# An explicit table of all operations in place of a list scheduler, in an attention and MLP kernel

## The chip, the core and the metric

The kernel runs on one core of one Trainium2 chip. The core has a matrix engine (TensorE, PE in the profile; its weight loads are PEld), a vector engine (VectorE, DVE), a scalar engine (ScalarE, ACT), a general one (GpSimd, POOL) and an engine that here only issues DMAs (SyncE, SP). Each works through its own queue in order. The metric is the time of one execution in microseconds of device time; lower is better.

## What is computed

Attention with a bias that a small network makes from the relative position, and then a two-layer MLP with a leaky activation over the concatenated heads. All is float32, and the constants in front of the random inputs are left out here:

```python
scores = scale * np.matmul(q, k.transpose(0, 1, 3, 2))          # B 4, H 8, S 576, D 64
rel = (pos[:, None] - pos[None, :]).astype(np.float32)
x = (np.log1p(np.abs(rel)) / np.log1p(np.maximum(pos[:, None], 1.0)))[..., None]
bias = np.maximum(x @ w1 + b1, 0.0) @ w2                         # hidden 32, one column per head
attn = softmax(scores + bias.transpose(2, 0, 1)[None])
out = np.matmul(attn, v)
...
h = x @ w_in                                                     # 2304 x 512 @ 512 x 2048
g = np.maximum(h, 0.0) + alpha * np.minimum(h, 0.0)
return g @ w_out                                                 # 2304 x 2048 @ 2048 x 512
```

## The kernel before

The program first makes a list of 2816 operations and then puts them in order. Each operation is one closure that issues one or a few instructions, with the engines on which it may run and an assumed duration for each, the buffers that it reads and writes, and a key.

The parts are these. Thirty-six bias tiles (`bias_tile`, "bias t"): for 4 x 4 positions each, four relu rows of 576 columns (L491 on DVE, L494 on ACT or L497 on POOL, tag "H"), a block of 16 matmuls with them (L506), an evacuation with scaling (L516 on ACT or L519 on DVE, tag "ev") and a store to a scratch array in DRAM. Eight weight pairs (`weights`, "w fp"): loads of 512 KB, unpacking of the input's 64-bit words with one shift (L678) and two combining steps on DVE (L681), maxima (L685, L686), casts to a high half in float16 (L700, L706, tag "wh") and the low half (L404). Turned q and k (`qk_turn`), the rows of v (`v_rows`). Thirty-two attention units (`unit`): scores (L613, L614), the row minimum on DVE (L808), the exponential on ACT (L811), the sum plus a small constant (L814, tag "ep"), its reciprocal (L816), and then for batch 0 a scaling (L831, tag "no"), turning on PE (L840) and evacuation (L850, tag "at"), for batches 1 to 3 a float16 high half (L821 on POOL, L822 on ACT, tag "nh"), the low half (L824) and a transposing DMA on SP into the tile `at`; then the product with v (L861, L869). Nine chunks of 256 tokens of the MLP (`chunk`, `layer_pair`): per pair of 128 columns the first layer (L939, 24 matmuls), two scalings (L946 on ACT, L947 on DVE), a cast (L950, tag "g0"), a subtraction (L951, tag "g1") and the second layer (L958); at the end of a chunk the output scaling (L920, L921, tag "mo") and the store.

Data are split into a high and a low float16 half, and three products of the halves stand for one product, so that most matmuls come in threes.

`Planner.plan` is a list scheduler: it goes through simulated time, and whenever an engine is free it takes the ready operation with the least key that finds free buffers, with assumed durations and an assumed slowing of DVE and POOL by one another (`SLOW`). The keys are the program's own plus an offset per part, all in the dictionary `ORDER`. The result fixes engine, buffer and place of every operation. `tc.manual_schedule` then issues them in that order, and waits on semaphores are made from the dependences. While the first MLP call isn't reached, PE gets fillers in planned gaps of over 600 ns: matmuls of 512 columns on a constant, into the tile H (L1012; 175 of them).

What sets the work around the change is thus the place of an operation in its engine's queue, the wait of its first instruction, and the buffer it was given: the small classes are two tiles S (and O as a third) and one tile A and H in PSUM, two float16 tiles `a` and two tiles `at`.

## Time and profile before

| | us |
|---|---|
| median of 3 runs | 737.98 (737.81 to 738.19) |
| profiled execution | 735.5 |
| its span | 733.7 |
| PE busy, of the span | 688.6 (94%) |
| DVE busy | 546.5 (74%) |
| ACT busy | 416.2 (57%) |
| POOL busy | 158.0 (22%) |

The span runs from the first instruction to the end of the last work; what lies around it makes up the rest of the profiled execution's time. Matmul records overlap, so a busy PE is not a PE at its peak. The share of an engine over the whole span is a mean over stages with different limits, so the views below are taken by stretch: busy time in windows, groups of instructions by line of code with the mean of one, who waited for whom, and the order in time. A wait that was for several engines stands under the one that came last.

### The profile page before, as it was taken

What the parts mean: (1) busy time and instruction counts of PE and PEld (TensorE: products, weight loads), DVE (VectorE), ACT (ScalarE), POOL (GpSimd) and SP (SyncE); (2) the same over time, 40 slices, a digit from 0 to 9 for tenths busy, and PEclk for the clock granted to TensorE, in tenths of its full rate; (3) what the DMA queues carried; (4) which work ended last, traced back from release to release, by engine and by line L of the source; (5) the groups of instructions that cost most, each with busy time, mean ns of one, the idle gap of its engine ahead of it and who ended that gap; (6) DMA issues with size and microseconds to landing.
All of it is one profiled execution on the core that took longest, in us unless ns stands there. A gap on an engine that the chain in (4) does not pass through costs nothing.

```text
span 733.7 us, 14984 instructions
## 1 busy us (share of the span) xinstructions
PE 688.6 (94%) x5508; PEld 421.8 (57%) x5508; DVE 546.5 (74%) x1267; ACT 416.2 (57%) x821; POOL 158.0 (22%) x191
## 2 busy tenths in 40 slices
PE   8888888988999999998999999999989999999997
PEld 3443334545656675655666666666656656666764
DVE  6999999899778987888987688777666775233332
ACT  3787777767667655645756666655454553223231
POOL 2367767623121211120210110000010111000000
PEclk9999989999999999999999999999999999999999
DMA  7999875756338996999999989979888896100000
GB/s 176 274 297 302 263 244 184 233 182 199 104 89 197 218 223 143 229 201 228 211 186 212 216 185 179 216 164 216 147 183 180 173 199 99 19 29 1 29 1 29
DMA packets 228361, 125.88 MB, mean 172 GB/s; under 512 B 204864, under 2 KB 204864, under 8 KB 228288
## 3 DMA queue, kind: packets, MB, share of 16 engines
q1 hardware_dynamic: 227952, 124.92, 73.0%
q8 instruction: 43, 0.70, 0.4%
q14 instruction: 30, 0.25, 0.1%
q10 hardware_dynamic: 336, 0.00, 0.0%
HBM read 74.17 MB, written 15.34 MB: 122 GB/s over the span
## 4 chain that ended last, share of the span: by engine, by line
PE 62%; DVE 21%; DMA 6%; issue 4%; ACT 3%; POOL 1%; SPq 1%; DVEq 0%; ACTq 0%; POOLq 0%
PE H L939 22%; PE O L958 21%; PE A L861 6%; PE S L614 5%; DVE fg L808 3%; DMA at<-a 3%; DVE a L824 2%; DVE five L681 2%; PE S L506 1%; DVE mg L947 1%; PE S L588 1%; DVE fg L519 1%; PE S L613 1%; DVE win L681 1%; PE A L869 1%
## 5 line engine op out<-in xcount | busy, mean ns | idle before, releaser
L958 PE MATMUL O<-wout,mg 128*128 128x512 f16 x864 | 200.8, 381 | 7.2 <-DVE st L808 4.6
L939 PE MATMUL H<-x,win 128*128 128x256 f16 x1728 | 200.7, 273 | 2.5 <-DVE mg L947 2.2
L939 PEld LDWEIGHTS <-win 128*128 128x128 f16 x1728 | 166.6, 98 | 35.7 <-issue 9.0
L811 ACT ACTIVATE fg<-fg,st 128x576 f32<-128x576 f32 x144 | 110.7, 770 | 64.8 <-DVE st L808 54.8
L958 PEld LDWEIGHTS <-mg 128*128 128x128 f16 x864 | 81.9, 98 | 102.7 <-issue 13.0
L947 DVE SCALAR_TENSOR_TENSOR mg<-H,sm,mg 128x256 f32<-128x256 f32 x144 | 64.3, 478 | 87.8 <-ACT mg L946 87.1
L821 POOL TENSOR_SCALAR a<-fg,st 128x576 f16<-128x576 f32 x55 | 47.9, 872 | 343.5 <-DMA at<-a 240.6
L946 ACT ACTIVATE mg<-H,sm 128x256 f32<-128x256 f32 x144 | 60.3, 469 | 96.1 <-PE H L939 95.3
L824 DVE SCALAR_TENSOR_TENSOR a<-fg,st,a 128x576 f16<-128x576 f32 x108 | 90.7, 841 | 13.8 <-ACT a L822 8.7
L808 DVE CUSTOM_DVE_ANT_0 fg<-S,fg 128x576 f32<-128x576 f32 x128 | 93.0, 752 | 7.9 <-PE S L614 6.2
L497 POOL TENSOR_SCALAR at<-cst,npsi 128x576 f32<-128x576 f32 x67 | 66.2, 996 | 49.4 <-PE S L506 36.2
L951 DVE TENSOR_TENSOR mg<-mg 128x512 f16<-128x512 f32 x72 | 50.1, 696 | 20.0 <-ACT mg L950 19.6
L950 ACT ACTIVATE mg<-mg 128x512 f16<-128x512 f32 x54 | 34.1, 631 | 40.4 <-DVE mg L947 39.0
L822 ACT ACTIVATE a<-fg,st 128x576 f16<-128x576 f32 x53 | 40.9, 773 | 26.8 <-DMA at<-a 24.6
L614 PE MATMUL S<-qk 64*128 64x288 f16 (+1 forms) x666 | 52.3, 285 | 0.8 <-DVE st L808 0.7
L861 PE MATMUL A<-at,five 128*64 128x256 f16 (+3 forms) x720 | 51.6, 288 | 0.4 <-DVE sm L632 0.4
L506 PE MATMUL S<-at,w2b 128*32 128x512 f32 (+1 forms) x464 | 48.6, 421 | 2.9 <-DVE fg L519 2.0
L494 ACT ACTIVATE at<-cst 128x576 f32<-128x576 f32 x54 | 39.4, 766 | 14.3 <-PE S L506 8.5
L1012 PE MATMUL H<-sm 128*128 128x512 f16 x175 | 45.8, 395 | 1.0 <-DVE sm L430 1.0
L861 PEld LDWEIGHTS <-five 128*64 128x64 f16 (+1 forms) x720 | 36.5, 109 | 15.7 <-issue 12.4
L614 PEld LDWEIGHTS <-qk 64*128 64x128 f16 (+1 forms) x720 | 31.9, 96 | 22.7 <-issue 17.2
L831 POOL TENSOR_SCALAR fg<-fg,st 128x576 f32<-128x576 f32 x36 | 30.1, 847 | 61.3 <-DVE st L816 34.0
(139 smaller groups left out, 754.7 us busy)
## 6 DMA issues: line engine op xcount, KB each, us to landing
fg<-scr SPq DMA_DIRECT2D x64, 576.0 KB, 4.8
scr<-fg SPq DMA_DIRECT2D x36, 288.0 KB, 4.4
x<-in_moe_w_in_dram SPq DMA_DIRECT2D x11, 512.0 KB, 4.5
x<-in_moe_w_out_dram SPq DMA_DIRECT2D x10, 512.0 KB, 5.3
fg<-scr SPq DMA_DIRECT2D x32, 144.0 KB, 4.8
out_dram<-mg SPq DMA_DIRECT2D x18, 256.0 KB, 3.0
five<-in_q_dram SPq DMA_DIRECT2D x32, 128.0 KB, 4.4
five<-in_k_dram SPq DMA_DIRECT2D x32, 128.0 KB, 3.3
```

Of the source, the lines that this page charges most:

```text
L497: nc.gpsimd.tensor_scalar(hb.t, R[:, lo:lo + S], 3.0e38, npsi[:, g:g + 1], op0=ALU.min, op1=ALU.max)
L506: nc.tensor.matmul(ps.t[32 * gl:32 * gl + 32, c:n], lhsT=w2b, rhs=hs[gl].t[:, c:n], start=True, stop=True)
L614: return [(lambda a, dst=dst, zq=zq, zk=zk, i=i: nc.tensor.matmul(dst(a), lhsT=tr16(qt)[at, 0, pr, zq, lo:lo + n], rhs=tr16(qt)[at, 1, pr, ...
L808: V(lambda x=x, sl=sl, st=st, ls=ls: nc.vector.tensor_tensor_reduce(out=in_halves(ls[x]()), in0=halves(sl[x].t), in1=in_halves(ls[x]()), s ...
L811: A(lambda x=x, st=st, ls=ls: nc.scalar.activation(ls[x](), ls[x](), AF.Exp, bias=st.t[:, x:x + 1], scale=-1.0, accum_out=st.t[:, 2 + x:3 ...
L824: V(lambda x=x, rec=rec, ls=ls, a16=a16: nc.vector.scalar_tensor_tensor(a16.t[:, 640:640 + S], ls[x](), rec(), a16.t[:, 0:S], op0=ALU.mult ...
L861: nc.tensor.matmul(ps.t[64 * hh:64 * hh + 64, 0:w], lhsT=v5[0:hi, zv, n, 2 * pr + hh, :], rhs=at16(at)[0:hi, 5 * za + n, 320 * hh:320 * hh ...
L939: nc.tensor.matmul(hb.t[:, f, :], lhsT=win[:, fp, zw, kb, P * f:P * f + P], rhs=x[:, zx, kb, :], start=(n == 0), stop=(n == 11))
L946: A(lambda f=f: nc.scalar.activation(gf(f), hb.t[:, f, :], AF.Copy, scale=cu[:, f:f + 1]), 470, ky, [hb, t_sig], [(g, f)])
L947: V(lambda f=f: nc.vector.scalar_tensor_tensor(gf(f), hb.t[:, f, :], cs[:, f:f + 1], gf(f), op0=ALU.mult, op1=ALU.max), 475, ky, [hb, t_si ...
L951: pl.op([("DVE", 690, lambda: nc.vector.tensor_tensor(gv(1), g.t, gv(0), op=ALU.subtract)), ("POOL", 1210, lambda: nc.gpsimd.tensor_tensor ...
L958: nc.tensor.matmul(ob.t[:, t, :], lhsT=gg.t[:, zg, f, P * t:P * t + P], rhs=wout[:, fp, zw, f, :], start=(first and f == 0 and (zg, zw) == ...
```

## The change

The list scheduler is removed. In its place stand three literal tables. `ISSUE` gives all 2816 operations in order by their number in the list, with ".1" or ".2" behind the number where a later of the operation's engines is taken; `SLOT` gives the buffer of each of the 1116 buffer uses; `IDLE` gives the fillers by operation and is empty. `plan` reads them. The operations themselves and their instructions are the same, apart from the engine. A flag `cont` is added to three kinds of operation; only the removed scheduler read it.

Counted in the table, against the engines of before (all other kinds keep their engine but for one or two):

| tag, lines | what | before | after |
|---|---|---|---|
| H, L491/L494/L497 | relu rows | ACT 61, DVE 9, POOL 74 | ACT 38, DVE 23, POOL 83 |
| ev, L516/L519 | bias evacuation | ACT 18, DVE 18 | ACT 33, DVE 3 |
| wh, L700/L706 | weight casts | ACT 24 | ACT 14, POOL 10 |
| z, L539 | small memsets | POOL 19, DVE 1 | POOL 12, DVE 8 |
| ep, L814 | sum plus constant | DVE 77, POOL 3 | DVE 36, POOL 44 |
| no, L831 | scaling, batch 0 | POOL 36 | POOL 32, DVE 4 |
| at, L850 | evacuation of turned tiles | ACT 36 | ACT 31, DVE 5 |
| nh, L821/L822 | high half, batches 1 to 3 | POOL 55, ACT 53 | POOL 78, ACT 30 |
| g0, L950 | cast | ACT 54, DVE 18 | ACT 36, DVE 36 |
| g1, L951 | subtraction | DVE 72 | DVE 34, POOL 38 |
| mo, L920/L921 | output scaling | DVE 15, ACT 3 | DVE 6, ACT 12 |
| fillers, L1012 | | PE 175 | 0 |

All small loads of the set-up are issued by ACT (13, before 7 and 6 by SP). On SP the load of a weight tile ("w 2") stands first, ahead of the constants, and DVE unpacks it ahead of its set-up steps. Among PE's 414 operations 335 keep their order, and none is more than 9 places from where it was; on SP some are up to 99 places away.

The diff, cut to its core (the tables are 95 and 16 lines long):

```diff
-ORDER = {
-    "keys": {
-        "init": -2208.04, "qk_0_0": 648.03, "bias_0": 106.57, "bias_1": 124.56, "bias_2": 28.45, "bias_3": -63.2, "bias_4": 34.22, "bias_5": -201.82,
...
-    "share": 5.541,
-    "queued": 20844316461613.4,
-}
+ORDER = {'keys': {}, 'offs': {}, 'prices': {}}
+ISSUE = """
+1 269 270 0 2 271 272 17 11.1 8.1 5.1 14.1 19 20 21 22 15.1 12.1 9.1 6.1 23 25 29 24 763.2 93.1 33 10.1 34 16.1 7.1 765.1 13.1 26 96.1 30 31 277 18.1
...
+SLOT = """
+0 0 1 1 0 0 2 2 4 0 1 2 0 4 3 5 0 1 0 0 2 3 0 1 0 4 0 4 2 1 0 5 4 0 1 2 1 3 1 2 0 4 0 3 3 5 0 6 1 0 3 0 1 2 1 2 5 4 0 1 0 0 2 4 6 0 0 1 3 0 1 2 0 1 2
...
+IDLE = """
+
+"""
...
     def plan(self):
-        Slots.used = set()
-
-        def backlog(e, o):
...
-        self.length = max(o.end for o in out)
-        out.sort(key=lambda o: (o.start, o.seq))
+        bufs = []
         for o in self.ops:
...
+            bufs += [b for b in o.bufs if b.slot is None]
+            for b in o.bufs:
+                b.slot = -1
+        for b, n in zip(bufs, SLOT.split(), strict=True):
+            b.slot = int(n)
+        out, place = [], {}
+        for x in ISSUE.split():
+            n, a = (x + ".0").split(".")[:2]
+            o = self.ops[int(n)]
+            o.eng, _, o.alt = o.alts[int(a)]
+            place[o] = len(out)
+            out.append(o)
...
         return out
...
-                   for nm, d, e in (("DVE", 175, nc.vector), ("POOL", 250, nc.gpsimd))], ky, [(st, 2 + x) for x in range(n)], [(st, 4)], tag="ep")
+                   for nm, d, e in (("DVE", 175, nc.vector), ("POOL", 250, nc.gpsimd))], ky, [(st, 2 + x) for x in range(n)], [(st, 4)], tag="ep", cont=True)
...
-    free, gaps = 0.0, {}
-    for o in ordered:
-        if o.eng == "PE":
-            if o.part.startswith("mlp"):
-                break
-            gaps[o.seq] = int(0.85 * (o.start - free) / 250) if o.start - free > 600 else 0
-            free = o.end - pl.LAT
+    gaps = {int(n): int(k) for n, k in (x.split(":") for x in IDLE.split())}
     with tc.manual_schedule():
         for o in ordered:
             for _ in range(gaps.get(o.seq, 0)):
```

## Rows read from the trace of the kernel before

**Rows 1.** Stretch, its length; busy PE, PEld, DVE, ACT, POOL; clock, DMA share, GB/s.

```profile
0.00:190.00 190.00, 162.96 (x1211) 78.15 (x1212) 171.51 (x357) 133.55 (x220) 100.13 (x112) 0.98 0.76 229
190.00:560.00 370.00, 358.47 (x3039) 233.67 (x3038) 296.16 (x744) 224.57 (x475) 49.13 (x69) 1.00 0.91 190
560.00:734.00 174.00, 167.17 (x1262) 109.94 (x1259) 78.88 (x168) 58.07 (x126) 8.74 (x10) 1.00 0.35 69
```

**Rows 2.** Timeline of PE: start us, duration us, the first call of the first layer.

```profile
189.60 2.79 PE L939 MATMUL H<-x,win 128*128 128x256 f16 x24
```

**Rows 3.** Waits of DVE, first 190 us: us in total, times, longest.

```profile
DVE sm L442 <- DMA sm<-in_b_dram: 2.9, 1, 2.9
DVE sm L438 <- DMA sm<-in_w_dram: 1.3, 1, 1.3
```

**Rows 4.** DVE by line, first 190 us: busy us, mean ns, idle before.

```profile
L681 DVE SCALAR_TENSOR_TENSOR five<-x,five 128x512 int32<-128x512 int32 x22 | 18.1, 824 | 0.6
...
L519 DVE TENSOR_SCALAR fg<-S,cst 128x576 f32<-128x576 f32 x16 | 13.9, 866 | 0.9 <-issue 0.6 <-PE S L506 0.3
L681 DVE SCALAR_TENSOR_TENSOR wout<-x,wout 128x512 int32<-128x512 int32 x10 | 9.3, 928 | 0.3
...
L491 DVE TENSOR_SCALAR at<-cst 128x576 f32<-128x576 f32 x8 | 4.7, 593 | 0.0
```

**Rows 5.** Single lines of code: shortest, median, longest ns, first and last start us.

```profile
L681 DVE SCALAR_TENSOR_TENSOR five<-x,five x22: 673/693/1181, 35.6 to 184.3; 128x512 int32<-128x512 int32 x22
L497 POOL TENSOR_SCALAR at<-cst,npsi x67: 736/951/1705, 8.7 to 139.9; 128x576 f32<-128x576 f32 x67
L814 DVE TENSOR_SCALAR st<-st x77: 130/160/640, 97.9 to 605.5; 128x2 f32<-128x2 f32 x61, 128x1 f32<-128x1 f32 x16
L814 POOL TENSOR_SCALAR st<-st x3: 192/192/193, 153.1 to 407.3; 128x2 f32<-128x2 f32 x3
```

**Rows 6.** The fillers alone (L1012), first 190 us, columns as above, PE and PEld.

```profile
0.00:190.00 190.00, 45.75 (x175) 15.54 (x175) 0.98 0.76 229
```

**Rows 7.** PE and its granted clock in single microseconds (busy, clock, DMA share, GB/s).

```profile
90.00:91.00 1.00, 0.00 (x0) 1.00 0.66 201
...
93.00:94.00 1.00, 1.00 (x7) 0.50 0.80 312
...
96.00:97.00 1.00, 1.00 (x6) 1.00 0.06 23
...
110.00:111.00 1.00, 1.00 (x8) 0.50 1.00 403
```

**Rows 8.** Timeline of PE: one bias block at full clock, one at half.

```profile
87.70 1.68 PE L506 MATMUL S<-at,w2b 128*32 128x512 f32 x16
...
93.42 2.15 PE L506 MATMUL S<-at,w2b 128*32 128x512 f32 x16
```

**Rows 9.** Waits of PE, 190 to 734 us, the largest of nine.

```profile
PE O L958 <- DVE st L808: 4.6, 2, 2.9
PE H L939 <- DVE mg L947: 2.2, 4, 1.0
```

**Rows 10.** Waits of POOL and ACT for the tile the transposing DMA reads.

```profile
POOL a L821 <- DMA at<-a: 240.6, 32, 30.2
...
ACT a L822 <- DMA at<-a: 24.6, 22, 3.7
```

**Rows 11.** Groups of MLP evacuations on DVE, whole span, columns as in rows 4.

```profile
L951 DVE TENSOR_TENSOR mg<-mg 128x512 f16<-128x512 f32 x72 | 50.1, 696 | 20.0 <-ACT mg L950 19.6
...
L921 DVE TENSOR_SCALAR mg<-O,sm 128x512 f32<-128x512 f32 x15 | 11.1, 748 | 8.3 <-PE O L958 8.3
...
L950 DVE CAST mg<-mg 128x512 f16<-128x512 f32 x18 | 7.7, 429 | 0.9 <-PE O L958 0.4
```

**Rows 12.** Timeline of the tail.

```profile
726.56 2.55 PE L958 MATMUL O<-wout,mg 128*128 128x512 f16 x11 [0.34 <-DVE mg L951]
729.14 1.41 DVE L921 TENSOR_SCALAR mg<-O,sm 128x512 f32<-128x512 f32 x2 [2.64 <-PE O L958]
```


## What was predicted before the change ran

> **What bounds the kernel now.** I read the busy times by stretch first [rows 1]. In the first 190 us VectorE (DVE) is busy 171.5 us, and it is the engine that waits least: 18.5 us in hundreds of small gaps, of which the two largest, 4.2 us together, are loads of the start [rows 3]. TensorE (PE) is busy 163.0 us there, but 45.75 us of that are fillers [rows 6], so its real work is 117 us of 190. The first call of the first MLP layer starts at 189.6 us [rows 2]. From there PE takes over: 358.5 of 370 us, then 167.2 of 174 us [rows 1], and all its waits behind 190 us come to 13.1 us, of which [rows 9] shows the two largest groups. So the time is a DVE stage of 190 us, whose length is that of DVE's own queue, and a PE stage of 540 us in which hardly more than 13 us can be won. Behind the last matmul 4.6 us remain, evacuations and the last store [rows 12].
>
> **The change part by part.** All counts are read off the table, against the engines that the trace of before shows. PE's own calls hardly move: of 414 none is listed more than 9 places from where it was, so the PE stage holds the same matmuls in nearly the same order. What changes is who evacuates, and when.
>
> *DVE's queue ahead of the first first-layer call.* The table lists 14 more bias rows there on DVE (593 ns each, [rows 4]): +8.3 us. It takes 15 bias evacuations away (866 ns, [rows 4]): -13.0 us. Five transposed tiles come from ACT; the trace has no such operation on DVE, so I bound it by the two kinds of row at hand, 593 ns (from SBUF) and 866 ns (from PSUM), and take 866, as it reads PSUM too: +4.3 us (3.0 to 4.3). The rest (four memsets and two other operations more, eight sums and a dozen small scalings fewer, 0.16 us each by [rows 5] for the small ones) is -1.5 us. Sum **-1.9 us**, all on the path, since DVE is the bound there.
>
> *The start.* The table puts the first weight tile's load ahead of all others on SP and its three integer operations ahead of DVE's small set-up steps. That fills some of the 4.2 us in which DVE waited [rows 3] (the three cost about 1.8 us), but the set-up then stands behind that load, and the constants' load behind it on SP too. Between -1.8 and +2 us; I take **0**.
>
> *DVE against GpSimd (POOL).* The weight unpacking (L681, 64 of them) has 673 ns as its shortest and 824 and 928 ns as its means in two of its groups [rows 4, 5]; POOL's bias rows have 736 ns as their shortest, 951 as their median and 1705 as their longest [rows 5]. Both grow where the two run side by side: over 64 the unpacking alone loses about 64 x 0.15 = 10 us. The table gives POOL more in this stage: 9 bias rows (0.95 us), 8 weight casts (no such row on POOL; 512 and 1024 columns by the bias row's 576 give 0.85 and 1.7 us, about 10 us in all), 8 sums (0.19, [rows 5]), less five memsets and three scalings: about +17 us on 100 [rows 1]. If meetings grow in that proportion, the 10 us become 12 and the other operations lose about 1 more. I take **+3 us**. Above it is bounded by all 17 us stopping DVE, below by the 10 us lost now, if the table keeps the two apart.
> The Trainium skill, "SBUF — State Buffer", section "Who interferes with whom", says that the second of the two to start stands still until the first has ended. By that alone the sum would take +17 here; the shortest and the median unpacking lie 20 ns apart in one group [rows 5], so many do not meet POOL at all, and the trace neither proves nor excludes the rule for those that do.
>
> *The fillers.* All 175 go (the third table is empty). They cost PE 45.75 us in a stretch in which it isn't the bound, so their end brings nothing by itself. What they bought is the clock: it fell to 0.50 twice in that stretch, before 93 and before 110 us, the first time after PE had stood still for a whole microsecond and more [rows 7], although fillers ran before and after. Two falls came with 27 us of idle PE (190 less 163.0, [rows 1]); without fillers PE idles 73 us. In proportion that is five falls, and as the fillers lay in the longest gaps I expect about a dozen (an estimate from these rows). At half clock a block of 16 bias matmuls took 2.15 us against 1.68 [rows 8], a ratio of 1.28. A dozen falls with one or two blocks each are about 8 us of PE time, most of it under DVE's queue; the part where DVE waits for a score or a bias tile counts. I take **+1.5 us** (0 to +8). If PE ran at half clock all through, 117 us would become 150 by that ratio, still under 190.
> The Trainium skill, "TensorE: Matmul & The Clock Gate", section "Loop structure matters more than you think", asks for no idle stretches between bursts of matmuls, and speaks against taking the fillers out. Were every real matmul twice as long, as its two clock levels suggest, 117 us would become 234 and the stage 44 us longer; that is a rival below.
>
> *The waits of PE behind 190 us.* They sum to 13.1 us, nearly all for DVE, as in the two groups of [rows 9], or for ACT's evacuations. The table takes from DVE behind the first first-layer call 38 subtractions (0.696), 9 output scalings (0.748) and 33 sums (0.16), and adds 18 casts (0.429) and some 5 us of smaller work [rows 5, 11]: -26.4 - 6.7 - 5.3 + 7.7 + 5 = -26 us of the 375 us it is busy there. ACT loses 23 attention scalings and 18 casts. A queue shorter by 7% doesn't end a wait by itself, but these waits lie where DVE is behind by one or two instructions. I take half: **-7 us** (0 to -13). What is late next is the transposing DMA (the DMA engines are busy 0.91 from 190 to 560 us, [rows 1]), which no part of the table makes faster.
>
> *POOL's queue behind 190 us.* The subtraction of a 128x512 pair has no row on POOL; by its bias row per element it would be 0.85 us, and twice that for two operands, 0.85 to 1.7 us. PE's next first-layer call of 2.8 us [rows 2] lies between, so the operation itself is covered. But POOL is in order, and its scaling waits for a tile that the transposing DMA frees: 32 times, 240.6 us [rows 10]. Now 24 sums and 20 subtractions stand directly behind such a scaling, and DVE's reciprocal and PE's second layer wait for them. ACT waited for the same tile 22 times, 1.1 us each [rows 10]. I take **+1.5 us** (0 to +12: half of the 44 late by 1.1 us, half of that seen by PE).
>
> *The tail.* The last cast moves to DVE and the wait of 0.34 us before the last matmuls [rows 12] goes: **-0.4 us**.
>
> The sum: -1.9 + 0 + 3 + 1.5 - 7 + 1.5 - 0.4 = -3.3 us. The profiled execution took 735.5 us (span 733.7); it becomes 732.2. The median of the runs is 737.98, 2.5 us over it, so the forecast is **734.7 us**.
>
> **The rivals.**
> - *POOL's queue holds the others up (slower).* Place: POOL behind 190 us. A scaling waits for its tile and a sum or subtraction stands behind it; it decides from the point where that wait is longer than the first-layer call that covers it. For it: 240.6 us of such waits and the 44 places. Against: in before POOL came early and simply waited, and the table can list a scaling later. Price 12 in place of 1.5: 745 us. Chance 0.17.
> - *DVE and POOL stop one another (slower).* Place: the first 190 us. The additional 17 us of POOL stop DVE fully: 734.7 - 3 + 17 = 748.7; half of it gives 740 to 743. For it: the spread of [rows 5]. Against: the many undisturbed ones. Chance 0.15. This is what the lock named above would do.
> - *The clock stays low (slower).* PE's real work doubles in the first stage: 738 + 44 = 782 us. Against it: at 96 us the clock was back after real matmuls [rows 7]. Chance 0.03.
> - *The table keeps POOL and DVE apart and PE's waits end (faster).* The 10 us of meetings go, and all 13.1 us of waits: 734.7 - 13 - 6 = 716; with half of it 725. For it: the table is free to place each operation. Chance 0.15.
> - *No change.* The moved work lies beside the bound, and what the stages win and lose is equal: 738 us. Chance 0.14.
>
> **How the numbers follow.** The forecast has 0.36, with a range of its own from 730 to 736.4. Faster by over 0.2% (which is about what a measurement of this kernel can tell from no change): 0.36 + 0.15 = 0.51; within 0.2% 0.14; slower 0.17 + 0.15 + 0.03 = 0.35. The range that leaves out no more than two in ten reaches from the middle of the fast rival to the price of POOL's queue: 721 to 747 us.
>
> **What would show it right or wrong.** The start of the first first-layer call, now 189.6 us: I expect 190 to 193; under 183 the fast rival holds, over 198 the meetings of DVE and POOL do, and the means of L681 tell. The granted clock in the first 190 us: about a dozen falls, mean 0.88 to 0.95. PE's waits behind that call: 6 us in place of 13. POOL's waits for the tile of the transposing DMA, and DVE's waits for POOL's sums: near zero if I am right, over 10 us if POOL's queue is the rival that holds. The forecast is wrong if the first stage moves by more than 8 us either way.

## The result: 748.2 us, slower by 1.4%

The changed kernel takes 748.18 us (median; 746.66 to 751.14) where the kernel before took 738.09 beside it: a ratio of 1.0138, 95% interval 1.0107 to 1.0170. I had forecast 734.7 with a range of 721 to 747. Sign and range were both wrong. The profiled execution took 746.66 us, its span 744.3, against 735.5 and 733.7 before.

The first place to look is the stretches, which answer [rows 1]; the columns are the same, and the third stretch is 11 us longer, as the span is.

```profile
0.00:190.00 190.00, 132.82 (x961) 62.92 (x961) 166.26 (x320) 110.22 (x182) 118.10 (x126) 0.89 0.71 216
190.00:560.00 370.00, 356.61 (x3026) 233.27 (x3026) 288.26 (x716) 205.68 (x450) 110.58 (x144) 1.00 0.91 190
560.00:745.00 185.00, 178.10 (x1350) 116.26 (x1347) 80.22 (x179) 62.18 (x135) 25.43 (x32) 1.00 0.37 78
```

In the first 190 us DVE has got through 320 instructions where it had done 357, in 166 us of work for 171. POOL is busy 118 us for 100. The granted clock is 0.89 for 0.98. From 190 to 560 us the clock is full, DVE carries 8 us less and POOL more than twice as much, as the table says. The timeline of PE, which answers [rows 2], gives the first first-layer call:

```profile
201.90 2.79 PE L915 MATMUL H<-x,win 128*128 128x256 f16 x24
```

It comes 12.3 us later (201.90 for 189.60). From there to the end of the span it is 542.4 us for 544.1, 1.7 us less: PE is busy 524.6 us for 526.0, as the kernel before had one more fall of the clock there (3.4 us at half), its gaps are 13.9 us for 13.5, and behind the last matmul there are 3.9 us for 4.6. The 0.6 us that are missing to 746.66 - 735.5 = 11.2 lie outside the span. So the whole loss is ahead of that call, and the questions are what the 12.3 us are, and why so little came back behind it. (Line numbers of the changed kernel are those of before less 24.)

Three things in that stage look guilty. DVE, by line, ahead of the call (busy us, mean ns | idle before), answering [rows 4]:

```profile
L657 DVE SCALAR_TENSOR_TENSOR five<-x,five 128x512 int32<-128x512 int32 x22 | 19.1, 870 | 0.5
L467 DVE TENSOR_SCALAR at<-cst 128x576 f32<-128x576 f32 x21 | 14.9, 723 | 5.7 <-PE S L482 5.6
L657 DVE SCALAR_TENSOR_TENSOR win<-x,win 128x512 int32<-128x512 int32 x10 | 9.3, 928 | 0.2
...
L657 DVE SCALAR_TENSOR_TENSOR wout<-mg,wout 128x512 int32<-128x512 int32 x6 | 6.1, 1024 | 0.2
```

The bias rows on DVE (L467) have a mean of 723 ns where [rows 4] had 593, and there are 21 for 8; 5.6 us of waiting for bias sums (PE S L482) stand ahead of them. I call *stretch* what the instructions of a kind took over the tenth part of that kind that was fastest in the kernel before, summed. Up to the call DVE's stretch is 32.2 us for 24.1, its idle time 24.6 for 18.5, and its remaining work 145.4 for 147.1 us (busy 177.6 and 171.2). Such a sum of stretch is good to about 1 us: it moves by so much with the way the fastest tenth is taken.

Second, PE's bias matmuls by line, up to the call, the kernel before and then the changed one:

```profile
L506 PE MATMUL S<-at,w2b 128*32 128x512 f32 x232 | 45.0, 620 | 2.9 <-DVE fg L519 2.0 <-ACT fg L516 0.4 <-DVE at L491 0.2
```

```profile
L482 PE MATMUL S<-at,w2b 128*32 128x512 f32 x232 | 59.6, 724 | 18.9 <-POOL at L473 7.5 <-ACT fg L492 5.0 <-DVE at L467 2.6
```

They overlap, so the busy time counts each microsecond once: 59.6 for 45.0. Part of that is the clock. The profile records six falls to half ahead of the call, 41 us together (before: two, 6.8 us). It has no record of the clock for the changed kernel's first 20.9 us, which the view of the stretches counts as full; but the wide bias matmuls (512 columns) took half clock's time there. Here they are up to 20.8 us, and then from 24 to 40 us (columns as in the rows above: busy us, mean ns | idle before):

```profile
L482 PE MATMUL S<-at,w2b 128*32 128x512 f32 x16 | 4.8, 1023 | 0.0
```

```profile
L482 PE MATMUL S<-at,w2b 128*32 128x512 f32 x38 | 9.1, 604 | 2.1 <-POOL at L473 2.0
```

Counted at half from the start, the mean of the first 190 us is 0.84 and not 0.89, and the time at half up to 62 us, which is the "about 61" in the expectation of e1 below. PE has nothing to do for the first 13.35 us of it. Third, the start: DVE's and PE's timelines of the changed kernel.

```profile
4.66 0.43 DVE L654 TENSOR_SCALAR win<-mg 128x512 int32<-128x512 int32 x1 [3.13 <-DMA mg<-in_moe_w_in_dram]
5.04 0.09 DVE L398 MEMSET w2b<- 128x32 f32 x1
...
13.06 0.24 DVE L421 TENSOR_SCALAR w2b<-w2b,sm 128x32 f32<-128x32 f32 x1 [2.08 <-DMA w2b<-in_w_dram]
```

```profile
13.48 1.06 PE L482 MATMUL S<-at,w2b 128*32 128x512 f32 x4
```

The memset of `w2b` stands behind the unpacking, which waits 3.13 us for the weight load; the four loads into `w2b` wait for the memset, and the first bias matmul comes at 13.48 us, 3.8 us later than before.

### The profile page after: what moved, and what is told of

Same layout as the page of the kernel before. It is cut to its first block, busy times and chain, and to the rows that moved or that the text cites. A ratio compares the mean times of both kernels' runs of the same rounds, so it can differ in the third digit from the quotient of the medians.

```text
span 744.3 us, 14558 instructions
## 1 busy us (share of the span) xinstructions
PE 667.5 (90%) x5333; PEld 412.4 (55%) x5333; DVE 534.7 (72%) x1213; ACT 378.1 (51%) x765; POOL 254.1 (34%) x301
## 4 chain that ended last, share of the span: by engine, by line
PE 61%; DVE 22%; issue 6%; POOL 4%; ACT 4%; DMA 3%; ACTq 0%; DVEq 0%; POOLq 0%; SPq 0%
PE H L915 22%; PE O L934 20%; PE S L590 5%; PE A L837 4%; DVE fg L784 3%; PE S L482 3%; DVE mg L923 2%; POOL fg L807 2%; DVE a L800 2%; PE S L816 2%; PE S L589 1%; DVE win L657 1%; DVE wout L657 1%; PE S L564 1%; ACT mg L922 1%
## 5 line engine op out<-in xcount | busy, mean ns | idle before, releaser
L915 PE MATMUL H<-x,win 128*128 128x256 f16 x1728 | 200.7, 273 | 3.8 <-DVE mg L923 3.6
L915 PEld LDWEIGHTS <-win 128*128 128x128 f16 x1728 | 166.6, 98 | 37.9 <-issue 12.0
L922 ACT ACTIVATE mg<-H,sm 128x256 f32<-128x256 f32 x144 | 65.6, 469 | 143.2 <-PE H L915 111.9
L934 PEld LDWEIGHTS <-mg 128*128 128x128 f16 x864 | 81.7, 98 | 99.9 <-issue 12.1
L923 DVE SCALAR_TENSOR_TENSOR mg<-H,sm,mg 128x256 f32<-128x256 f32 x144 | 67.1, 480 | 97.2 <-ACT mg L922 96.9
L797 POOL TENSOR_SCALAR a<-fg,st 128x576 f16<-128x576 f32 x78 | 64.1, 822 | 158.2 <-DMA at<-a 86.0
L800 DVE SCALAR_TENSOR_TENSOR a<-fg,st,a 128x576 f16<-128x576 f32 x108 | 90.9, 844 | 26.5 <-POOL a L797 16.5
L928 POOL TENSOR_TENSOR mg<-mg 128x512 f16<-128x512 f32 x38 | 46.7, 1229 | 168.0 <-ACT mg L926 86.6
L784 DVE CUSTOM_DVE_ANT_0 fg<-S,fg 128x576 f32<-128x576 f32 x128 | 93.6, 751 | 13.1 <-PE S L590 9.6
L473 POOL TENSOR_SCALAR at<-cst,npsi 128x576 f32<-128x576 f32 x74 | 76.2, 1040 | 43.1 <-PE S L482 32.8
L482 PE MATMUL S<-at,w2b 128*32 128x512 f32 (+1 forms) x464 | 63.9, 485 | 18.9 <-POOL at L473 7.5
L482 PEld LDWEIGHTS S<-at,w2b 128*32 128x32 f32 x464 | 19.8, 122 | 61.5 <-issue 25.6
L790 POOL TENSOR_SCALAR st<-st 128x2 f32<-128x2 f32 (+1 forms) x44 | 15.6, 354 | 79.3 <-ACT fg L787 77.7
L492 ACT ACTIVATE fg<-S,cst 128x576 f32<-128x576 f32 x30 | 24.7, 825 | 26.6 <-PE S L482 20.0
L470 ACT ACTIVATE at<-cst 128x576 f32<-128x576 f32 x34 | 25.9, 767 | 17.0 <-PE S L482 15.2
```

Source lines behind the costliest of these rows:

```text
L473: nc.gpsimd.tensor_scalar(hb.t, R[:, lo:lo + S], 3.0e38, npsi[:, g:g + 1], op0=ALU.min, op1=ALU.max)
L482: nc.tensor.matmul(ps.t[32 * gl:32 * gl + 32, c:n], lhsT=w2b, rhs=hs[gl].t[:, c:n], start=True, stop=True)
L784: V(lambda x=x, sl=sl, st=st, ls=ls: nc.vector.tensor_tensor_reduce(out=in_halves(ls[x]()), in0=halves(sl[x].t), in1=in_halves(ls[x]()), s ...
L797: pl.op([("POOL", 775, lambda x=x, rec=rec, ls=ls, a16=a16: nc.gpsimd.tensor_scalar(a16.t[:, 0:S], ls[x](), rec(), 1.0, op0=ALU.mult, op1= ...
L800: V(lambda x=x, rec=rec, ls=ls, a16=a16: nc.vector.scalar_tensor_tensor(a16.t[:, 640:640 + S], ls[x](), rec(), a16.t[:, 0:S], op0=ALU.mult ...
L915: nc.tensor.matmul(hb.t[:, f, :], lhsT=win[:, fp, zw, kb, P * f:P * f + P], rhs=x[:, zx, kb, :], start=(n == 0), stop=(n == 11))
```

## The experiments

All kernels but one are tables of the changed kernel's form, so that the order, the engines, the buffers and the fillers can be set one by one; "the kernel before" is then the list scheduler's own result, written as a table. Times are the median and the ratio to the kernel before beside it; "call" is the start of the first first-layer call in the profile. All 1116 buffer choices are the same in the tables of the two kernels (e1 and the changed one), so the buffers have no part in the loss. Each call and each view is from one execution, and executions of the kernel before lie between 731 and 742 us; a microsecond more or less in the accounts below can be chance.

| run | call, us | median, us | ratio, 95% interval |
|---|---|---|---|
| before | 189.6 | 736.4 to 738.1 | |
| after | 201.9 | 748.18 | 1.0107 to 1.0170 |
| e1 before, no fillers | 190.3 | 739.21 | 1.0013 to 1.0064 |
| e2 after, fillers of before | 210.4 | 755.85 | 1.0233 to 1.0306 |
| e3 after, start of before | 204.7 | 749.12 | 1.0149 to 1.0216 |
| e4 before, all first-stage engines of after | 199.1 | 747.57 | 1.0122 to 1.0199 |
| e5 before, its H engines alone | 198.2 | 745.53 | 1.0066 to 1.0146 |
| e6 before, the other engines alone | 197.6 | 746.52 | 1.0075 to 1.0165 |
| e7 after, first-stage engines of before | 244.3 | 794.90 | 1.0730 to 1.0831 |
| e8 before, later engines of after | 189.9 | 743.49 | 1.0058 to 1.0113 |
| e9 after, own fillers | 197.3 | 743.27 | 1.0078 to 1.0113 |
| e10 e9 with start of before | 201.4 | 745.59 | 1.0101 to 1.0137 |
| e11 after, short POOL rows | 181.2 | 725.15 | 0.9829 to 0.9868 |
| e12 before, short POOL rows | 174.9 | 722.15 | 0.9785 to 0.9823 |
| e13 e11 with own fillers | 174.7 | 718.50 | 0.9699 to 0.9769 |
| e14 e3 with own fillers | 201.1 | 745.92 | 1.0073 to 1.0136 |
| e15 before, own fillers | 188.4 | 735.75 | 0.9961 to 1.0002 |

### e1 and e2: the fillers taken from one and given to the other

```diff
 e1 (the table of the kernel before)
-IDLE = """ 30:27 767:4 97:3 90:3 648:4 ... 839:4 """    # 175 in 33 places
+IDLE = """ """
 e2 (the changed kernel; operation 3, the constant, moved to the front of ISSUE)
-IDLE = """ """
+IDLE = """ 30:27 767:4 97:3 90:3 648:4 ... 839:4 """
```

> The kernel before with its order, engines and buffers, all unchanged, but without the 175 empty matmuls. Three theories share out the 12.3 us that the changed kernel loses ahead of its first first-layer call (201.9 us for 189.6). The clock: without fillers TensorE stood at its lower clock for about 61 us of that stage, and DVE, ACT and POOL waited for longer bias matmuls; then this kernel loses most of it too: first call at 198 to 202 us, 746 to 750 us in all, and long stretches of granted clock 0.5. The meetings of DVE and POOL (7.4 us more of stretched DVE instructions): nothing of that is here, call at 189 to 191, 738 us. The start (first bias matmul 3.8 us later): nothing here either, 738 us.

> The changed kernel with the 175 empty matmuls of the kernel before, ahead of the same TensorE operations in the same numbers; the constant that they read is set first of all on DVE (0.06 us). The clock: granted clock near 1.0 in the first stage, the bias matmuls back at about 421 ns, first call at 190 to 193 us, 736 to 739 us in all. The meetings of DVE and POOL: the clock comes back, but the call stays at 197 to 202, 744 to 748 us. The start: the same, 744 to 748 us. If the causes add up, it lies between, at 740 to 744.

Both theories of a single cause lose here. Without fillers the kernel before falls to half clock five times in its first stage (mean 0.92; its first 13.1 us have no record either, and PE works there from 8.55 us), and its call moves by 0.7 us:

```profile
0.00:190.00 190.00, 138.93 (x1032) 68.35 (x1032) 168.82 (x355) 133.74 (x220) 98.47 (x112) 0.92 0.76 229
```

DVE has done 355 instructions in 190 us where it had done 357. The little loss is a net one: up to the call DVE idles 21.2 us for 18.5 and is busy 169.1 us for 171.1. DVE waits more and is stretched less, and the two nearly cancel. The whole time grew by 0.4% (0.13 to 0.64). But the same 175 fillers in the changed kernel made it slower by 8.5 us at the call, and the clock stayed at 0.89. They stand ahead of the same operations as before, and there those are now waited for. DVE's waits up to 200 us, in e2:

```profile
DVE at L467 <- PE S L482: 8.6, 6, 3.4
DVE sm L451 <- PE A L450: 4.2, 4, 2.8
DVE fg L784 <- PE S L589: 3.3, 2, 2.5
```

The first of them was 5.6 and the second 2.3 us without fillers. A filler fits the gap that it was made for, and e2 says nothing of the price of the clock. It needed e9.

### e3: the start of the kernel before

```diff
-1 269 270 0 2 271 272 17 11.1 8.1 ...
+0 5 8.1 3 1 4 11 14.1 2 6.1 17 ... 32 269 270 271 272 763.2 ...   # 0 to 32 first, as before
```

> The changed kernel with the 33 operations of the setup (memsets, small loads, the scaling of the constants) first in the order and on the engines of the kernel before, so that the unpacking of w_in no longer stands ahead of them; nothing else is moved, and there are no fillers. The start: first bias matmul at about 9.7 us for 13.5, first first-layer call 3.5 to 4.7 us earlier at about 198, 743.5 to 744.7 us. The clock, or the meetings: the first bias matmul moves, but the call stays within 1.5 us of 201.9, 747 to 748 us.

The first bias matmul came at 9.4 us, 4.1 us earlier, and the call at 204.7, 2.8 us later. A start that was 3.8 us late was thus not what cost 3.8 us, but the clock was lower in this run than in the changed kernel (51 us recorded at half between 0 and 200 us, for 41), so it could not settle the matter; e10 and e14 take it up.

### e4 to e8: the engines alone

```diff
 e4: before, 136 operations of the first stage on after's engines (H, ev, at, ep, z, wh, no, qk)
 e5: the 89 H rows of them;  e6: the other 47;  e7: after, the 136 turned back
 e8: before, 186 operations behind the first stage on after's engines (nh, ep, g0, g1, mo, ...)
-... 763 764.2 ... 89.1 ...        # e4
+... 763.2 764 ... 89.2 ...        # number.engine; order, buffers and fillers stay
```

> The kernel before, with its order, buffers and fillers, and with the engine choices of the changed kernel for the operations of the first stage alone (136 of them: the H rows of the bias tiles, their evictions, clears, weight halves, and the normalisation and eviction of the first batch's attention). The meetings of DVE and POOL: DVE's stretched time rises by 7 us and the first call comes at 195 to 198 us, 744 to 747 us in all. The clock, or the start: fillers and start are those of before, the call stays at 188 to 192, 736 to 740 us. A rival to all of them, an order that no longer fits its engines: over 750.

> The kernel before, its order, buffers and fillers, with the changed kernel's engines for the H rows of the bias tiles alone (89 rows move: 38 from ACT to POOL, 10 from ACT to DVE, 25 from POOL to ACT, 10 from POOL to DVE, 6 from DVE to POOL). That all 136 moves of the first stage together cost 9.5 us at the first call (199.1 us) leaves open which of them do. Theory of the rows: rows that take about 1 us on POOL where ACT took 0.72 make the tiles of biases late, and DVE waits for their sums; then most of it is here, call at 195 to 199, 744 to 747 us. Theory of the other moves (the additive step of the softmax on POOL, evictions of transposes on DVE): call at 189 to 192, 737 to 739 us.

> The counterpart: the kernel before with the changed kernel's engines for the other 47 operations of the first stage that move (15 evictions of bias tiles from DVE to ACT, 5 evictions of transposes from ACT to DVE, 8 additive steps of the softmax from DVE to POOL, 8 weight halves from ACT to POOL, clears), the H rows left where they were. Theory of the rows: call at 188 to 192, 736 to 739 us, or a little faster than before, since DVE sheds 10 us of evictions. Theory of the other moves: DVE waits for POOL's sums and for the late weight halves, call at 195 to 199, 743 to 747 us.

> The changed kernel, its order and buffers, without fillers, with the 136 engine choices of the first stage turned back to those of the kernel before. If the engines alone carry the loss of 12.3 us, call at 189 to 193 and 736 to 740 us (the kernel before without its fillers took 739). If the loss comes from engines that do not fit the order they run in, in either direction, this one loses as well: call at 197 or later, 745 us or more. If the order has a part of its own: between, call at 194 to 197.

> The kernel before, its order, buffers and fillers, with the changed kernel's engines for the operations behind the first stage alone (186 of them: rounding steps of the second and later batches between POOL and ACT, additive steps to POOL, g0 and g1 of the first layer between DVE, ACT and POOL, output scalings). The changed kernel took 542.4 us from its first call to the end for 544.1. If these moves carry that gain, the stretch takes 541 to 543 us here, 734 to 737 us in all. Rival: on an order that is not theirs they cost, the 1.2 us subtraction on POOL above all, which stands between DVE's copy and the second layer: 740 us or more. Third: nothing, 738 us.

e4 looked like the answer: 9.5 of the 12.3 us. It is not. The rows alone cost 8.6 us and the other moves alone 8.0, and both together 9.5, so neither has a price of its own. And e7, which should have brought the kernel back to 738 us, was 47 us slower than the changed kernel. Its DVE waits up to the call:

```profile
DVE wout L378 <- ACT wout L674: 22.0, 7, 8.2
DVE fg L493 <- issue: 10.3, 2, 6.1
DVE st L788 <- ACT fg L785: 7.4, 6, 2.3
DVE w2b L419 <- DMA w2b<-in_w_dram: 5.8, 1, 5.8
```

The weight halves went back to ACT (L674), stood there at the place that POOL's order had given them, and DVE waited 22 us for them. An order on in-order queues is made for its choice of engines, and whoever changes one of the two alone measures the misfit. e4 shows it on a smaller scale: DVE's idle time there rose by 8.6 us (18.5 to 27.1) and its stretch by 1.1 us only, whereas in the changed kernel the stretch rose by 8.1. The loss of e4 is of the same size and of another kind. It also says something of the meetings: the same engines stretch DVE by 8.1 us more in the changed kernel's order and by 1.1 us in the order of before, so the choice of engines alone doesn't make them. e8 likewise took 551.5 us behind the call for 544.1: PE's gaps there grew by 4.0 us (17.5 for 13.5), and the clock stood at half for 10.2 us in place of 3.4. So it doesn't tell what the later moves are worth in their own order.

### e9: fillers in the changed kernel's own gaps

```diff
-IDLE = """ """
+IDLE = """ 30:45 287:2 634:6 111:3 178:8 69:2 ... 793:9 839:3 """   # 153 in 26 places; operation 3 first, as in e2
```

> The changed kernel with 153 empty matmuls in its own gaps: ahead of each of the 26 TensorE operations of the first stage that came over 0.6 us after the one before it, as many as 85% of that gap holds (45 of them ahead of the first operation, at 13.4 us). The fillers of the kernel before had stood at other places here, and the kernel got slower by them (call at 210.4 us). Theory of the clock: once the fillers lie in the gaps, the granted clock is 0.96 or more ahead of the call, the stretched time of the bias matmuls falls from 37 us to under 12, and the call comes at 190 to 195 us, 735 to 741 us in all. Theory of the engines and their order: the clock rises, the call stays at 198 to 203, 744 to 749 us, as the kernel before lost only 0.7 us at its call without fillers.

```profile
0.00:190.00 190.00, 157.63 (x1135) 71.86 (x1137) 171.31 (x327) 112.49 (x185) 121.62 (x129) 0.99 0.74 223
```

```profile
L657 DVE SCALAR_TENSOR_TENSOR five<-x,five 128x512 int32<-128x512 int32 x22 | 19.5, 888 | 0.5
L467 DVE TENSOR_SCALAR at<-cst 128x576 f32<-128x576 f32 x21 | 15.7, 763 | 3.5 <-PE S L482 3.5
```

Now the clock is held (0.99), the wide bias matmuls fall from 724 to 603 ns in the mean, and the call comes 4.6 us earlier, at 197.3; 743.27 us in all for 748.18. Neither theory had the number: the call lies between the two ranges. The clock is worth 4.6 us here. DVE idles 5.1 us less up to the call, 2.1 of them in its waits for bias sums (3.5 for 5.6) and 1.6 in those for a maximum that PE turns (L451, 0.7 for 2.3). 7.7 us remain. With the clock held, DVE's idle time is 19.5 us, nearly what it was before the change (18.5). What is left is busy time: 178.2 us for 171.2, its stretch 33.1 for 24.1.

### e11 and e12: POOL's rows made short

```diff
-nc.gpsimd.tensor_scalar(hb.t, R[:, lo:lo + S], 3.0e38, npsi[:, g:g + 1], op0=ALU.min, op1=ALU.max)
+nc.gpsimd.tensor_scalar(hb.t[:, 0:64], R[:, lo:lo + 64], 3.0e38, npsi[:, g:g + 1], op0=ALU.min, op1=ALU.max)
...
+        nc.gpsimd.memset(at1[:, 0:5 * S], 0.0)
+        nc.gpsimd.memset(fg[:, n_f - 2:n_f], 0.0)
```

> The changed kernel, with its order, engines and buffers and no fillers, but the H rows on POOL write 64 of their 576 columns (the rest stays what a memset at the start left, so the biases are left out there): POOL's 83 rows take about 0.2 us for 1.0, and DVE hardly meets them. Theory of POOL's rows (stretched DVE instructions, and bias tiles that wait for the slowest row): the stretched time of DVE falls from 32 us to under 14, and the call comes at 178 to 186 us; and the gap to the kernel before with the same cut shrinks from 12.3 us to under 4. Theory that the order and the clock are what is lost: both kernels gain about as much from the cut, and the gap stays at 9 to 14 us.

> The kernel before with the same cut of its 74 rows on POOL (the biases are left out there; scheduler, order, engines and fillers as they were). It gives the mark for the run before this one: stretched time of DVE from 24 us to under 10, call at 174 to 182 us by the theory of POOL's rows, and 4 us or less ahead of the changed kernel with the cut; by the other theory 9 to 14 us ahead of it. If POOL's rows matter to neither, the call stays at 187 to 190 us.

DVE, by line, up to the call, e11 first and then e12:

```profile
L657 DVE SCALAR_TENSOR_TENSOR five<-x,five 128x512 int32<-128x512 int32 x22 | 16.9, 768 | 0.5
L467 DVE TENSOR_SCALAR at<-cst 128x576 f32<-128x576 f32 x21 | 10.6, 523 | 5.8 <-PE S L482 5.6
```

```profile
L681 DVE SCALAR_TENSOR_TENSOR five<-x,five 128x512 int32<-128x512 int32 x22 | 16.4, 747 | 0.6
L681 DVE SCALAR_TENSOR_TENSOR win<-x,win 128x512 int32<-128x512 int32 x10 | 7.0, 700 | 0.3
```

DVE's rows fall to 523 ns in the mean, the groups of the unpacking to between 700 and 768, the stretch from 32.2 to 9.6 us (after) and from 24.1 to 5.8 (before). The call moves by 20.7 us in the changed kernel and by 14.7 in the one before, so full rows on POOL cost the changed kernel 6.0 us more. Short rows take away much of POOL's work at once, so this is what the full rows cost in all: by stopping DVE, and by coming late. The gap between the two shrank from 12.3 to 6.3 us, not below 4 as the theory of the rows had it, and not to 9 or more as its rival: the clock was still low in e11 and not in e12.

### e13: both at once

```diff
 e11 and
+IDLE = """ ... """    # 123 empty matmuls in e11's own gaps
```

> The changed kernel with POOL's rows cut to 64 columns (the biases are left out there) and 123 empty matmuls in its own gaps, found in the trace of the run with the cut alone. Of the 12.3 us at the first call, fillers in its own gaps gave back 4.6 and the short rows took 6.0 more than they took from the kernel before; whether the two add up, and what the 1.7 left over is, stays open. If they add up: the call at 175.5 to 178 us (181.2 less 4.6), within 3 us of the kernel before with the same cut (174.9), 719 to 722 us in all. If the clock costs only where POOL's rows hold the tiles up: the call stays at 179.5 to 182, 723 to 726 us, and a part of the loss is neither.

```profile
174.71 2.79 PE L914 MATMUL H<-x,win 128*128 128x256 f16 x24
```

The kernel before with short rows, e12, has it here:

```profile
174.94 2.79 PE L939 MATMUL H<-x,win 128*128 128x256 f16 x24
```

With short rows and the clock nearly held (one fall of 6.8 us), the two kernels reach the call within 0.2 us of each other. That gives an account of the 12.3 us: 4.6 are the clock (201.9 to 197.3, e9), 7.9 are what full rows on POOL cost the changed kernel more than the one before (197.3 less 174.7, against 189.6 less 174.9: 22.6 for 14.7), and -0.2 is all the rest in sum, the start, the work moved on and off DVE and POOL's weight casts included. Of the 7.9 us 5.8 are busy time of DVE (177.8 to 154.5 us from e9 to e13, 171.1 to 153.6 from before to e12), which is stretch, as DVE's instructions are the same; 2.0 are idle time. The clock gave 6.5 us with short rows and 4.6 with full ones. Taken in the other order the account is thus 6.0 for the rows and 6.5 for the clock: the rows are 6 to 8 us and the clock 4.6 to 6.5.

### e10 and e14: the start again

```diff
 e10: e9 with operations 0 to 32 first;  e14: e3 with 134 empty matmuls in e3's own gaps
```

> The same with the 33 operations of the setup first, in the order and on the engines of the kernel before (27 empty matmuls ahead of the first operation). Without fillers that start brought nothing: call at 204.7 us for 201.9, but with more of the stage at the lower clock. Theory of the start: with the clock held, the first bias matmul at about 9.7 us brings the call 3 to 4.7 us ahead of the run without it. Theory that the start is hidden: within 1 us of it, since DVE then waits for the weights instead.

> The changed kernel with the setup of the kernel before first, and 134 empty matmuls in the gaps that this very order showed in its run without fillers. The run before with this start had fillers in the gaps of another order, fell to the lower clock again, and so told nothing of the start. With the clock held (0.97 or more ahead of the call): if the start is worth its 3.8 us, the call comes at 193 to 195 us, 739 to 741 us in all. If DVE's queue takes that time up again at the weights, the call stays at 196.5 to 199 us as with fillers alone, 742 to 745 us. If the setup first does harm, 200 or more.

e10 had its fillers in gaps of another order and is of little use alone, but e14, with its own, has the call at 201.1, 3.8 us later than e9. The clock was not held as hoped (0.96). The timelines of e14, DVE and PE, show where the early start goes:

```profile
12.35 0.43 DVE L654 TENSOR_SCALAR win<-mg 128x512 int32<-128x512 int32 x1 [1.43 <-DMA mg<-in_moe_w_in_dram]
12.82 1.42 DVE L657 SCALAR_TENSOR_TENSOR win<-mg,win 128x512 int32<-128x512 int32 x2
14.15 0.94 DVE L467 TENSOR_SCALAR at<-cst 128x576 f32<-128x576 f32 x2
```

```profile
9.68 1.05 PE L482 MATMUL S<-at,w2b 128*32 128x512 f32 x4 [0.21 <-POOL at L473]
15.15 2.13 PE L482 MATMUL S<-at,w2b 128*32 128x512 f32 x12 [4.42 <-DVE at L467]
```

The first four matmuls run at 9.68 us. The next ones wait 4.42 us for a row on DVE, which stands behind the unpacking, which now waits for a weight load that was issued later. The other twelve of the tile's sixteen matmuls then run at half clock (2.13 us; the clock fell at 13.9 us for 10.2 us). So the setup put first alone moved the wait and gained nothing here. As the clock fell again, what the start is worth by itself isn't shown. A table with both the early start and that row ahead of the unpacking wasn't tried.

### e15: the kernel before with its own fillers

```diff
-IDLE = """ 30:27 767:4 97:3 90:3 648:4 ... 839:4 """    # 175 in 33 places, from the scheduler's plan
+IDLE = """ 30:28 767:3 97:2 90:2 43:2 ... 839:3 """    # 191 in 42 places, from its trace
```

> The kernel before, its order, engines and buffers, with its fillers taken anew from its own trace: 191 empty matmuls ahead of the 42 TensorE operations that came over 0.6 us after the one before them, for 175 ahead of 33 by the scheduler's plan. A candidate to beat both kernels. By the theory that the clock costs this kernel little (its call moved 0.7 us when all fillers went): within 0.2% of the kernel before, call at 188.5 to 190 us. By the rival that the two falls left in its first stage cost what they cost the changed kernel: 1 to 2 us faster.

The first stage has no fall left, and the call comes at 188.4, 1.2 us earlier. The median is 735.75 us beside 737.8, a ratio of 0.9981 whose interval, 0.9961 to 1.0002, just holds 1. It is the fastest complete kernel of this study, and that it beats the kernel before isn't shown.

## Why the prediction was wrong, step by step

The sum had -3.3 us, the profiled execution shows +11.2. By its own terms:

*What bounds the kernel.* Right: the time was lost in DVE's stage, and PE's stage kept its length to 1.7 us. The call moved by 12.3 us, over the 8 us that I had named as the sign of being wrong.

*DVE's queue, -1.9 us.* Right, as far as it goes: DVE's work without stretch is 147.1 us before and 145.4 after.

*The start, 0 (-1.8 to +2).* No loss of it shows at the call (e13 leaves -0.2 us for it and all else together), but its mechanism was wrong: I priced the constants' load behind the weight load and missed that the `w2b` memset stands behind the unpacking and four loads behind that memset, 3.8 us at the first bias matmul. That nothing of it would arrive at the call, I hadn't argued, and no run shows the start by itself.

*DVE against POOL, +3 us (-10 to +17).* The mechanism was right and was even a rival with a sign of its own (a call "over 198"); the size was 7.9 us by e9 and e13 (6.0 in the other order of the account). The step that failed is "if meetings grow in that proportion", in three ways. First, its base was short: I counted the 10 us that the unpacking loses, but by the measure above all of DVE's instructions lost 24.1 us there in the kernel before, and 17 in 100 of that is 4 us, not 3. Second, DVE's stretch grew by 8.1 us, a third, where POOL's busy time grew by 22% (99.9 to 122.1 us, up to a later call). Third, I priced DVE's new rows and the evacuations that left it by their means, as if the two were alike. They aren't. In the kernel before, shortest, median and longest ns of an evacuation (it reads PSUM) and of a row (it reads SBUF), and then the rows of the changed kernel:

```profile
L519 DVE TENSOR_SCALAR fg<-S,cst x16: 854/865/906, 13.7 to 91.2; 128x576 f32<-128x576 f32 x16
L491 DVE TENSOR_SCALAR at<-cst x8: 505/514/1006, 10.3 to 130.3; 128x576 f32<-128x576 f32 x8
```

```profile
L467 DVE TENSOR_SCALAR at<-cst x21: 507/537/1030, 9.5 to 103.5; 128x576 f32<-128x576 f32 x21
```

The evacuations take the same time whether POOL works or not (14 of 18 ran beside a POOL instruction: 867 ns in the mean, the other four 866). The rows don't: of the changed kernel's 23, the six without a POOL instruction beside them took 508 ns, the other 17 774. So the table took 15 instructions off DVE that POOL doesn't stretch and gave it 14 that it does: DVE's rows went from 0.7 to 4.5 us of stretch, the unpacking from 64 x 0.16 to 64 x 0.20. In e9 the rows take 763 ns each, in e13, where POOL's are short, 526. How the 7.9 us divide between the rows that came to POOL, those that came to DVE and the new order isn't shown; e4, with the same engines in the order of before, has only 1.1 us more stretch. The Trainium skill, "SBUF — State Buffer", section "Who interferes with whom", says that of two instructions of these engines that need the ports they share the second stands still until the first has ended; by that I had put +17 beside my +3, as if all that POOL gained met such instructions. The 7.9 us lie between.

That the measured 748.2 us equals the full price of this rival, 748.7, is luck. The meetings took about half of its 17 us, and without the clock's 4.6 us the call would have stayed at 197.3 (e9), under the sign of 198.

*The fillers, +1.5 us (0 to +8).* Measured 4.6 (e9). The mean clock in the view, 0.89, lies in the forecast of 0.88 to 0.95, but only because the first 20.9 us count as full; at half they make it 0.84. The failed step is "a dozen falls with one or two blocks each": there were six behind the start, but one of them lasted from 85.7 to 102.8 us, they make 41 us at half, and the start came on top. The prediction had priced no such start. The price of a block was short as well: the 1.68 us of [rows 8] were a slow one, as blocks at full clock went down to 1.18 us in the kernel before (at 25.62 us), and a wide bias matmul takes about 0.60 us at full clock and 1.06 at half, a ratio of 1.76 and not 1.28. Nor is the price the same in both orders. The kernel before lost 0.7 us at the call for 24 us more at half (e1, 30.7 for 6.8 us recorded), the changed one 4.6 for 38 us more (41.0 for 3.4 in e9), each with a start at half besides. The changed kernel's DVE has 23 rows that wait for a free tile, that is for the matmuls of the tile before; these waits are 2.1 of the 5.1 us that DVE idles less in e9. The Trainium skill, "TensorE: Matmul & The Clock Gate", section "Loop structure matters more than you think", spoke against taking the fillers out, and these runs bear it out for the changed kernel and hardly for the one before. The full rival (782 us) was far off.

*The waits of PE, -7 us.* This is the other large miss: 13.1 us before, 13.1 us after. PE's waits behind the call (us, times, longest), the largest of ten, answering [rows 9]:

```profile
PE H L915 <- DVE mg L923: 3.6, 7, 0.8
PE O L934 <- ACT mg L896: 2.9, 4, 1.2
PE O L934 <- DVE mg L900: 2.6, 2, 1.8
PE S L590 <- DVE st L784: 1.5, 2, 1.0
```

The 4.6 us for the softmax (L808 there) are gone, as are a few others. In their place PE waits for ACT's output scalings (L896), which the table moved off DVE, and longer for DVE's evacuation of the first layer (3.6 us for 2.2), which itself waits for ACT's evacuation of the same tile: 96.9 us (L923 on ACT L922) for 87.1 before. DVE is busy 357 us there for 375, so 18 us are gone where I had counted 26, and the waits didn't end. The step that failed is "a queue shorter by 7%" and the half that I took of it: DVE wasn't late for want of time. It stood behind ACT, and ACT behind PE's own first layer (L922 on PE's L915, 111.9 us for 95.3 before). Of the 1.7 us that were won behind the call, for 5.9 forecast with the two terms that follow, none comes from these waits: 1.5 are the clock, 0.7 lie behind the last matmul, and the gaps took 0.4 back.

*POOL's queue, +1.5 us.* Its mechanism is in the trace and off the path. POOL's waits for the tile are 86.0 us for the 240.6 of [rows 10]; neither near zero, as I had written, nor a harm:

```profile
POOL a L797 <- DMA at<-a: 86.0, 36, 8.7
```

```profile
DVE a L800 <- POOL a L797: 16.5, 20, 2.6
...
DVE st L792 <- POOL st L790: 4.4, 6, 1.6
```

DVE waited 4.4 us for POOL's sums and 16.5 for its scalings (5.0 before), PE 0.5 us for POOL altogether.

*The tail, -0.4 us.* The reason was wrong: the wait of 0.34 us is still there, and one of 0.78 us for ACT's scaling came in behind it. What did win 0.7 us is the part behind the last matmul: one output scaling on ACT (0.69 us) stands there where DVE did two (1.41 us, [rows 12]).

```profile
736.93 1.25 PE L934 MATMUL O<-wout,mg 128*128 128x512 f16 x5 [0.34 <-DVE mg L927]
738.96 1.46 PE L934 MATMUL O<-wout,mg 128*128 128x512 f16 x6 [0.78 <-ACT mg L896]
```

So of the 14.5 us between forecast and result, by the first order of the account, 4.9 are the meetings (7.9 for 3), 3.1 the clock (4.6 for 1.5), 4.2 the part behind the call, 1.7 what DVE's queue should have won and the rest of the stage took back, and 0.6 lies outside the span. Every bound of a term that could be measured held; the range of the sum didn't, since its terms came out on their slow sides together. I had summed middle values as if the unknowns were independent. In the first stage two of them may have one cause: the table takes rows from ACT, which had time (133 us busy, 116 after), and gives them to POOL and DVE, which stretch each other and then wait for the tiles. That is argued and not shown: no run puts the rows back on ACT in an order made for it.

## What to carry to other kernels

Where two engines stretch each other, look at the spread of each kind of instruction before pricing a swap of one kind for another by their means. Here DVE's rows from SBUF ran from 505 to 1006 ns and its evacuations from PSUM from 854 to 906, in the trace of before already. An order on in-order queues, its choice of engines and its fillers belong together: taken over alone, fillers cost 8.5 us, engines 8 to 42 us at the same call, so a part's price has to be measured by removing a cause (a held clock, short rows) and not by swapping a column of the table. Where the clock has no record, the matmuls' own durations tell it. A wait ends with what the waiting engine itself stands behind, so look one step further up before giving half of a group of waits away.

## What the runs showed of the hardware that was not expected

- A POOL row of 64 columns isn't a ninth of one of 576. In e12, shortest, median, longest ns:

```profile
L497 POOL TENSOR_SCALAR at<-cst,npsi x67: 308/428/1529, 8.7 to 124.9; 128x64 f32<-128x64 f32 x67
```

  It was 736, 951 and 1705 ns for the full row [rows 5]. I had expected 0.2 us. From 308 for 64 columns and 736 for 576 the fixed part is about 255 ns (an estimate from these two), and POOL is stretched by DVE in turn: the 25 short rows beside which none of DVE's kinds that stretch ran took 308 to 315 ns, the other 49 656 in the mean, and the longest began 0.5 us into a DVE instruction of 1.54 us (L641) and ended 0.5 us behind it.
- The subtraction of a 128x512 pair on POOL takes 1152 ns at least and 1229 in the mean (38 of them), in the bound of 0.85 to 1.7 us; a sum over 128x2 takes 192 ns in the median, and up to 1040.
- TensorE's lower clock had no price of its own here: 24 us more of it in the first stage cost 0.7 us at the call in one order (e1 against before), and 38 us more 4.6 us in another (after against e9), each with a start at half besides.
- An evacuation of 128x576 from PSUM on DVE isn't stretched by POOL (854 to 906 ns, and most ran beside a POOL instruction); a row of the same size from SBUF, 505 ns at least, took up to 1030.
